# When a guard's flag is made: between the last two adds, or after them

## The chip, the cores and the metric

The kernel runs on one core of one Trainium2 chip. Its time is device microseconds of one execution, the median of several runs. Beside the times there is one profiled execution, from which every duration below is read. Engines are named TensorE (PE, its weight loads PEld), VectorE (DVE), ScalarE (ACT), GpSimd (POOL) and SyncE (SP); a "q" behind the name (SPq) marks what the engine's sequencer does: waits, branches, DMA issues and loads of a register.

## The reference

For x of 2048 tokens by 512 (bfloat16), xn = layernorm(x), and the output is the sum of three parts:

```
x
+ attention(xn)   32 heads of 16, causal, a window of 256 tokens, softmax, then wo
+ mixer(xn)       z = gelu(xn @ w_in); z1, z2 = halves of z (688 each)
                  g = w_sp @ layernorm(z2) + b_sp;   (z1 * g) @ w_out
```

## The kernel before

The tokens are tiles of 128 (`NB` = 16). A first stage normalizes x, transposes it and makes the mixer's z; a second one works through attention and the rest of the mixer, in an order written out by hand (`ORDER`): each word of it takes a few matmuls from the generators `q_work` (projections), `g_work` (w_sp times z2) and `f_work`, or one step of attention (`do_scores`, `do_mask`, `pv`, `normalize`).

`f_work(t, c0)` makes the output of token tile t: six matmuls with `w_out` (L479) and four with `wo` (L486) into one bank, then VectorE adds x to it (L491), and a store goes out (L495). The last tile, t = 15, is done in two halves of 256 columns; the second half's store is issued by ScalarE, every other by SyncE. The order ends with `f10 f10 f10`: tile 14, then the two halves of tile 15.

Attention takes the exponent without subtracting a row's maximum. Whether that was safe is checked: `check_sums` compares the reciprocals of all the sums with two bounds; for the last group it reduces to one number for each partition (`low1`, L628), and a DMA of SyncE's (L632) brings these 128 numbers into one row on one partition, kept in `rows`. After the whole order the guard follows: VectorE reduces that row (L813) and makes `flag`, 0 or 1 (L816); `nc.values_load` (L819) has each of the five engines load the flag into a register, a `TENSOR_LOAD` in its queue; and `tc.If(again > 0)` (L825) has each engine compare and branch.

Where the flag is 1, `attention_with_maximum` makes all of the output again by a second path, with a maximum subtracted, in loops. With these inputs it isn't taken: each engine jumps over it. Each semaphore that the second path would count up is counted up instead on the way around it: one `EVENT_SEMAPHORE` (L825) on TensorE, VectorE, ScalarE and GpSimd, and eight on SyncE, one for each DMA semaphore, each waiting first until all earlier DMAs on it have landed. Then the kernel ends (L850): SyncE waits for all the semaphores, and two barriers follow.

All engines run their queues in order. SyncE's last work ahead of the guard are three stores (tiles 13 and 14, first half of 15); ScalarE's is the store of the second half.

Of the kernel before, what the change touches and what calls it, by code (L numbers as in the profile page):

```python
# [8 lines left out]
P = 128  # L9
BF = mybir.dt.bfloat16  # L10
F32 = mybir.dt.float32
ACT = mybir.ActivationFunctionType
ALU = mybir.AluOpType

S_TOK = 2048
D = 512
# [9 lines left out]
NB = S_TOK // P  # L26
# [47 lines left out]
def kernel(  # L74
# [12 lines left out]
    nc = tc.nc  # L87
    x2 = A_x.flatten_outer_dims()
    out2 = out.flatten_outer_dims()
# [22 lines left out]
    flag = pers.tile([P, 1], mybir.dt.int32, name="flag")  # L112
    wspp = ctx.enter_context(tc.tile_pool(name="wspp", bufs=2))
    sm = ctx.enter_context(tc.tile_pool(name="sm", bufs=4))
# [44 lines left out]
    with ExitStack() as actx:  # L159
# [20 lines left out]
        for half in range(2):  # L180
            for k, eng in ((0, nc.sync), (1, nc.scalar)):
# [3 lines left out]
                    out=w_in_sb[:, :, f0 : f0 + HALF], in_=w_in_v[:, :, f0 : f0 + HALF]  # L185
# [5 lines left out]
        with nc.allow_non_contiguous_dma(reason="tiny bias gather"):  # L191
# [3 lines left out]
            out=w_out_sb[:, 0:5, :], in_=B_w_out[0:640, :].rearrange("(c p) n -> p c n", p=P)  # L195
# [5 lines left out]
        for _ in range(WARM):  # L201
# [7 lines left out]
            out=hmask[:],  # L209
            in_=ident[:].rearrange("p (s e d) -> p e s d", s=4, e=2),  # L210
            axis=mybir.AxisListType.XY,
# [11 lines left out]
        for h in range(2):  # L223
            part = slice(h * KB, h * KB + KB)
            nc.gpsimd.affine_select(
                out=maskFD[part, 0, :], in_=maskFD[part, 0, :], pattern=[[-1, KB]],
# [3 lines left out]
                out=maskFD[part, 1, :], in_=maskFD[part, 1, :], pattern=[[1, KB]],  # L230
# [231 lines left out]
    def load_xo(t):  # L462
        xos[t] = cp.tile([P, D], BF, name="xo", bufs=4)
        nc.sync.dma_start(out=xos[t][:], in_=x2[t * P : (t + 1) * P, :])
# [4 lines left out]
    def f_cols(t):  # L469
        return D // 2 if t == NB - 1 else D  # L470

    def f_work(t, c0):
        if c0 == 0 and t + 2 < NB:
            load_xo(t + 2)
        xo = xos[t]
        w = f_cols(t)
        fo = ps_x.tile([P, 512], F32, name="fo", tag="f")
        for ch in range(NFC):
            nc.tensor.matmul(  # L479
                fo[:, 0:w], lhsT=uTs[t][:, ch, :], rhs=w_out_sb[:, ch, c0 : c0 + w],  # L480
                start=(ch == 0), stop=False,
            )
            yield
        q0 = t % 2 * P
        for c in range(NC):
            nc.tensor.matmul(  # L486
                fo[:, 0:w], lhsT=oTs[t // 2][:, c, q0 : q0 + P], rhs=wo_sb[:, c, c0 : c0 + w],
                start=False, stop=(c == NC - 1),
            )
            yield  # L490
        nc.vector.tensor_tensor(  # L491
            out=xo[:, c0 : c0 + w], in0=fo[:, 0:w], in1=xo[:, c0 : c0 + w], op=ALU.add
        )
        eng = nc.scalar if c0 > 0 else nc.sync
        eng.dma_start(out=out2[t * P : (t + 1) * P, c0 : c0 + w], in_=xo[:, c0 : c0 + w])  # L495

# [138 lines left out]
    def attention_with_maximum(gctx):  # L635
# [5 lines left out]
        def turn(out, src, k):  # L641
            pt = ps_x.tile([P, k, P], BF, name="pt", tag="f")
            for c in range(k):
                nc.tensor.transpose(
                    out=pt[:, c, :], in_=src[:, c * P : (c + 1) * P], identity=ident[:]
                )
            nc.vector.tensor_copy(out=out[:], in_=pt[:])
# [9 lines left out]
            out=band[:], in_=band[:], pattern=[[1, NK]],  # L657
# [3 lines left out]
            out=band[:], in_=band[:], pattern=[[-1, NK]],  # L661
# [7 lines left out]
        with tc.For_i(0, NG, 1) as G:  # L669
            qx = gen.tile([P, 2, S_TOK], BF, name="qx")  # L670
            for b in range(4):
                nc.vector.tensor_copy(
                    out=qx[:, :, b * 512 : b * 512 + 512],
                    in_=qpad[b][:, bass.ds(G, 1), :, :].rearrange("p o e q -> p (o e) q"),
                )
            nc.vector.tensor_copy(
                out=kx[:, KW:], in_=kT[:, bass.ds(G, 1), :].rearrange("p o k -> p (o k)")
            )
            nc.vector.tensor_copy(
                out=vx[:, 2:, :], in_=v_y[:, :, bass.ds(G * VG, VG)]  # L680
            )
            with tc.For_i(0, NB, 1) as t:
# [3 lines left out]
                    out=keep, in0=band[:], in1=valid[:, bass.ds(t * P, NK)], op=ALU.mult  # L686
                )
                nc.vector.tensor_scalar(
                    out=minus, in0=keep, scalar1=1.0, scalar2=NEG,
                    op0=ALU.subtract, op1=ALU.mult,  # L690
                )
                nc.vector.tensor_scalar(
                    out=keep, in0=keep, scalar1=SM_SCALE, scalar2=None, op0=ALU.mult
# [6 lines left out]
                    out=qw.rearrange("p (e q) -> p e q", e=2), in_=qx[:, :, bass.ds(t * P, P)]  # L700
                )
                nc.vector.tensor_copy(out=vw, in_=vx[:, bass.ds(t, 3), :])
                op = ps_s.tile([P, 2, 512], F32, name="op", tag="S")[:, 0, 0 : 8 * VW].rearrange(
                    "p (h w) -> p h w", w=VW)
                for hh in range(8):
# [13 lines left out]
                        out=p[:], in_=sc, func=ACT.Exp, bias=top[:], scale=1.0  # L719
# [3 lines left out]
                    for k in range(3):  # L723
# [8 lines left out]
                    out=oa[:, bass.ds(t, 1), bass.ds(G * P, P)].rearrange(  # L732
                        "p o (h d) -> p (o h) d", d=DH),
                    in0=op[:, :, 0:DH], in1=rs[:].unsqueeze(2).to_broadcast([P, 8, DH]),
                    op=ALU.mult,
                )

        with tc.For_i(0, NB, 1) as t:
            row0 = t * P
            xo = cp.tile([P, D], BF, name="xo", bufs=4)  # L740
            nc.sync.dma_start(out=xo[:], in_=x2[bass.ds(row0, P), :])
            ws = wspp.tile([P, NB, P], BF, name="wspT")
            nc.sync.dma_start_transpose(out=ws[:], in_=B_w_sp[bass.ds(row0, P), :])
            u = cp.tile([P, UPAD], BF, name="u")
            nc.gpsimd.memset(u[:, FH:UPAD], 0.0)
            for j in range(2):
                gf = ps_x.tile([P, 512], F32, name="gf", tag="f")
                for c in range(NB):
                    nc.tensor.matmul(
                        gf[:, 0:HALF], lhsT=ws[:, c, :],  # L750
                        rhs=z2n[:, c, j * HALF : (j + 1) * HALF],
                        start=(c == 0), stop=(c == NB - 1),
                    )
                nc.vector.scalar_tensor_tensor(
                    out=u[:, j * HALF : (j + 1) * HALF], in0=gf[:, 0:HALF],
                    scalar=b_all[:, bass.ds(t, 1)],
                    in1=z1[:, bass.ds(t, 1), j * HALF : (j + 1) * HALF].rearrange(
                        "p o f -> p (o f)"),
                    op0=ALU.add, op1=ALU.mult,
                )  # L760
            uT = cp.tile([P, NFC, P], BF, name="uT", bufs=4)
            turn(uT, u, NFC)
            oT = cp.tile([P, NC, P], BF, name="oT1", tag="u")
            ot = cp.tile([P, D], BF, name="ot1", tag="uT", bufs=4)
            nc.vector.tensor_copy(
                out=ot[:], in_=oa[:, bass.ds(t, 1), :].rearrange("p o d -> p (o d)")
            )
            turn(oT, ot, NC)
            fo = ps_x.tile([P, 512], F32, name="fo", tag="f")
            for c in range(NFC):  # L770
                nc.tensor.matmul(
                    fo[:], lhsT=uT[:, c, :], rhs=w_out_sb[:, c, :], start=(c == 0), stop=False
                )
            for c in range(NC):
                nc.tensor.matmul(
                    fo[:], lhsT=oT[:, c, :], rhs=wo_sb[:, c, :],
                    start=False, stop=(c == NC - 1),
                )
            nc.vector.tensor_tensor(out=xo[:], in0=fo[:], in1=xo[:], op=ALU.add)
            nc.sync.dma_start(out=out2[bass.ds(row0, P), :], in_=xo[:])  # L780

    rows = []
    masks = [(J, g, i) for J, g in pairs for i in range(3)]
    units = list(pairs)
    load_cross(0)
    work = {
        "q": [(4, q_work(b, i)) for b, i in qkv_list],
        "g": [(NB, g_work(t, j)) for t in range(NB) for j in range(2)],
        "f": [(NFC + NC, f_work(t, c0)) for t in range(NB) for c0 in range(0, D, f_cols(t))],
    }  # L790
    left = 0
    for step in ORDER.split():
# [16 lines left out]
            if left == 0:  # L809
                assert next(unit, None) is None  # L810
    assert not (left or groups or masks or units or later or any(work.values()))
    low = sm.tile([P, 1], F32, name="low")
    nc.vector.tensor_reduce(  # L813
        out=low[0:1, :], in_=rows[0][0:1, :], axis=mybir.AxisListType.X, op=ALU.min
    )
    nc.vector.tensor_scalar(  # L816
        out=flag[0:1, :], in0=low[0:1, :], scalar1=0.5, scalar2=None, op0=ALU.is_lt
    )
    again = nc.values_load(  # L819
        flag[0:1, 0:1], min_val=0, max_val=1,  # L820
        skip_runtime_bounds_check_because="a comparison gives 0 or 1",
    )
    late_ctx.close()
    ep_ctx.close()
    with tc.If(again > 0):  # L825
        with ExitStack() as gctx:
            attention_with_maximum(gctx)

# [26 lines left out]
```

## Time and profile before

| | |
|---|---|
| median of three runs | 258.57 us (258.11 to 258.86) |
| profiled execution | 258.24 us, its span 256.4 us |
| granted TensorE clock | 1.000 |
| busy share of the span | TensorE 97%, ScalarE 74%, VectorE 70%, GpSimd 6% |
| instructions | 9109 |
| DMA | 25.38 MB, of it 0.60 MB of instructions |

The span runs from the first to the last instruction of the program; the time of an execution has some 1.8 us around it. Starts are counted from the span's start. A group of instructions is shown with its line, engine, operation and count, then the shortest, middle and longest duration in ns and when the first and last of them started. The chain of waits goes back from the last piece of work to what released it, and is shown in order of time: start, duration, what. The view of the DMA queues gives packets, MB and the time that the packets took as a share of 16 DMA engines over the stretch asked for; its line "DMA" cuts that stretch into 40 slices and shows the busy share in tenths.

### The profile page before, as it was taken

To read this page: it belongs to the slowest core of one execution; us is meant where nothing else is said; L and a number is where in the kernel's file an instruction comes from. 1 tells how busy PE (TensorE), PEld (TensorE's weight loads), DVE (VectorE), ACT (ScalarE), POOL (GpSimd) and SP (SyncE) were. 2 spreads that over 40 slices of the span, in tenths; PEclk is the share of its full clock that TensorE was granted. 3 is DMA by queue.
4 is the path that set the end of the run, shared out by engine and by line. 5 is a ranking of instruction groups with operands and counts; after the bars stand their busy time and mean duration, and the time that the engine had idled before them with its cause. 6 is when DMAs were issued, how large, how long until landed. Compare 5 with 4: busy or idle time off the path is not lost.

```text
span 256.4 us, 9109 instructions
## 1 busy us (share of the span) xinstructions
PE 249.9 (97%) x4053; PEld 137.4 (54%) x4053; DVE 178.8 (70%) x370; ACT 190.7 (74%) x228; POOL 16.6 (6%) x52
## 2 busy tenths in 40 slices
PE   6999999999999999999999999999999999999993
PEld 2665555555555455464555564556465546465552
DVE  4796997885566758844679857385577877488983
ACT  2777536546546998989898889898988888986800
POOL 4120311211010100000000000000000000000000
PEclk9999999999999999999999999999999999999999
DMA  6994020026201206396843936465469193563032
GB/s 206 393 243 146 0 64 20 0 51 140 58 0 42 66 4 115 72 140 112 153 72 71 187 70 111 93 117 115 41 151 155 48 150 80 117 108 64 20 95 68
DMA packets 65786, 25.38 MB, mean 99 GB/s; under 512 B 53664, under 2 KB 65232, under 8 KB 65744
## 3 DMA queue, kind: packets, MB, share of 16 engines
q1 hardware_dynamic: 64256, 23.74, 44.4%
q10 hardware_dynamic: 1488, 1.03, 1.4%
q8 instruction: 32, 0.52, 0.9%
q14 instruction: 10, 0.08, 0.1%
HBM read 8.41 MB, written 2.10 MB: 41 GB/s over the span
## 4 chain that ended last, share of the span: by engine, by line
PE 96%; DVE 1%; DMA 1%; POOL 0%; issue 0%
PE gf L443 32%; PE zp L292 15%; PE S L580 10%; PE fo L479 9%; PE S L523 8%; PE pj_o L129 6%; PE fo L486 6%; PE pj_f L129 5%; PE pj_f L147 3%; PE pj_o L147 3%; DMA xt<-in_A_x_dram 1%; PE tp L282 1%; DVE stats L240 1%; POOL rs L250 0%; DVE xo L491 0%; DVE xn L268 0%
## 5 line engine op out<-in xcount | busy, mean ns | idle before, releaser
L589 ACT ACTIVATE E<-S 128x1024 bf16<-128x1024 f32 x152 | 141.2, 1025 | 16.1 <-PE S L580 15.8
L443 PE MATMUL gf<-z2n,wspT 128*128 128x344 bf16 x512 | 86.5, 310 | 0.0
L443 PEld LDWEIGHTS <-wspT 128*128 128x128 bf16 x512 | 45.5, 98 | 32.3 <-issue 11.6
L608 DVE TENSOR_TENSOR E<-E,maskFD 128x1024 bf16<-128x1024 bf16 (+2 forms) x48 | 38.4, 808 | 5.9 <-ACT E L589 5.4
L292 PE MATMUL zp<-w_in_sb,xnT 128*128 128x344 bf16 x256 | 41.7, 309 | 0.0
L292 PEld LDWEIGHTS <-xnT 128*128 128x128 bf16 x256 | 24.9, 98 | 15.1
L580 PE MATMUL S<-qpad,kT 32*64 32x512 bf16 (+3 forms) x960 | 31.9, 309 | 0.0
L530 DVE STREAM_TRANSPOSE ot<-S 128x1024 f32<-128x1024 f32 x16 | 19.9, 1244 | 16.7 <-PE S L523 16.5
L449 DVE SCALAR_TENSOR_TENSOR u<-gf,b_all,z 128x344 bf16<-128x344 f32 x32 | 18.3, 571 | 17.9 <-PE gf L443 15.6
L479 PE MATMUL fo<-w_out_sb,uT 128*128 128x512 bf16 (+1 forms) x102 | 24.4, 367 | 0.0
L299 ACT ACTIVATE z<-zp 128x688 bf16<-128x688 f32 x16 | 11.9, 745 | 15.1 <-PE zp L292 15.0
L580 PEld LDWEIGHTS <-kT 32*64 32x64 bf16 x960 | 10.8, 102 | 21.2 <-issue 20.2
L523 PE MATMUL S<-E,v_y 64*32 64x256 bf16 (+2 forms) x960 | 21.8, 231 | 0.0
L523 PE MATMUL S<-E,vx 64*32 64x256 bf16 (+3 forms) x960 | 21.8, 232 | 0.0
L523 PEld LDWEIGHTS <-vx 64*32 64x32 bf16 x960 | 18.4, 90 | 4.1 <-issue 3.7
L523 PEld LDWEIGHTS <-v_y 64*32 64x32 bf16 x960 | 19.2, 90 | 0.6 <-issue 0.6
L299 ACT ACTIVATE z2n<-zp 128x688 bf16<-128x688 f32 x16 | 11.9, 745 | 10.1 <-PE zp L292 10.1
L129 PEld LDWEIGHTS <-wqkv 128*128 128x128 bf16 x128 | 12.5, 98 | 12.4
L129 PE MATMUL pj_o<-xnT,wqkv 128*128 128x512 bf16 x72 | 18.5, 379 | 0.0
L140 DVE TENSOR_SCALAR qpad<-qt,hmask 128x512 bf16<-128x512 bf16 x32 | 9.7, 345 | 11.4 <-ACT qt L138 11.4
L486 PE MATMUL fo<-wo_sb,oT 128*128 128x512 bf16 (+1 forms) x68 | 17.3, 368 | 0.0
L491 DVE TENSOR_TENSOR xo<-fo,xo 128x512 bf16<-128x512 f32 (+1 forms) x17 | 11.1, 654 | 8.4 <-PE fo L486 8.1
(60 smaller groups left out, 197.2 us busy)
## 6 DMA issues: line engine op xcount, KB each, us to landing
xo<-in_A_x_dram SPq DMA_DIRECT2D x16, 128.0 KB, 3.5
out_dram<-xo SPq DMA_DIRECT2D x15, 128.0 KB, 2.2
vx<-v_y SPq DMA_DIRECT2D x16, 102.0 KB, 3.2
xt<-in_A_x_dram SPq DMA_DIRECT2D x3, 512.0 KB, 9.7
wqkv<-in_A_wqkv_dram SPq DMA_DIRECT2D x1, 1536.0 KB, 10.5
w_in_sb<-in_B_w_in_dram ACTq DMA_DIRECT2D x2, 344.0 KB, 5.8
w_in_sb<-in_B_w_in_dram SPq DMA_DIRECT2D x2, 344.0 KB, 6.0
w_out_sb<-in_B_w_out_dram SPq DMA_DIRECT2D x1, 640.0 KB, 5.6
```

Source lines behind the costliest of these rows:

```text
L129: nc.tensor.matmul(pt[:], lhsT=wqkv[:, c, w0 : w0 + P], rhs=xnT[:, c, t0 : t0 + 512], start=(c == 0), stop=(c == NC - 1),)
L292: nc.tensor.matmul(zp[:, j, 0:HALF], lhsT=xnT[:, c, n * P : (n + 1) * P], rhs=w_in_sb[:, c, f0 : f0 + HALF], start=(c == 0), stop=(c == NC ...
L299: nc.scalar.activation(out=dst.rearrange("p (j f) -> p j f", j=2), in_=zp[:, :, 0:HALF], func=ACT.Gelu_apprx_tanh,)
L443: nc.tensor.matmul(gf[:, 0:HALF], lhsT=wspT[t][:, c, :], rhs=z2n[:, c, j * HALF : (j + 1) * HALF], start=(c == 0), stop=(c == NB - 1),)
L449: nc.vector.scalar_tensor_tensor(out=u[:, j * HALF : (j + 1) * HALF], in0=gf[:, 0:HALF], scalar=b_all[:, t : t + 1], in1=z1[:, t, j * HALF ...
L479: nc.tensor.matmul(fo[:, 0:w], lhsT=uTs[t][:, ch, :], rhs=w_out_sb[:, ch, c0 : c0 + w], start=(ch == 0), stop=False,)
L486: nc.tensor.matmul(fo[:, 0:w], lhsT=oTs[t // 2][:, c, q0 : q0 + P], rhs=wo_sb[:, c, c0 : c0 + w], start=False, stop=(c == NC - 1),)
L523: nc.tensor.matmul(o[32 * s : 32 * s + 32, h, q0 : q0 + ni * KB], lhsT=v, rhs=Et[part, s, e, c0 : c0 + ni * KB], start=(i == 0), stop=(i = ...
L530: nc.vector.transpose(out=ot[:].rearrange("p h b j -> p (h b j)"), in_=o[:].rearrange("p h c -> p (h c)"))
L580: nc.tensor.matmul(o.rearrange("p (e q) -> p e q", e=2)[:, :, c0 - b0 : c0 - b0 + ni * KB], lhsT=kT[32 * s : 32 * s + 32, 2 * g + h, k0 : ...
L589: nc.scalar.activation(out=Et[:, 2 * i : 2 * i + 2, :, b0 : b0 + w].rearrange("p s e q -> p (s e) q"), in_=S[i][:].rearrange("p s (e q) -> ...
L608: nc.vector.tensor_tensor(out=v, in0=v, in1=mask, op=ALU.mult)
```

## The change

The reduce and the compare that make the flag move from behind the whole order into `f_work`: for the last half tile they are issued after its matmuls and ahead of its add. The load of the flag by the five engines moves there too, behind that add and ahead of that store's issue. So in each queue: VectorE has reduce, compare, add, load; ScalarE the load, then the store; TensorE the load behind its last matmul; SyncE behind its last store. In the second path two lines change: the load of x and the store of the output in its last loop go from SyncE's queue to ScalarE's, which then holds three DMAs of that path, with the transposes it had.

```diff
@@ f_work
             yield
+        last = t == NB - 1 and c0 + w == D
+        if last:
+            low = sm.tile([P, 1], F32, name="low")
+            nc.vector.tensor_reduce(
+                out=low[0:1, :], in_=rows[0][0:1, :], axis=mybir.AxisListType.X, op=ALU.min
+            )
+            nc.vector.tensor_scalar(
+                out=flag[0:1, :], in0=low[0:1, :], scalar1=0.5, scalar2=None, op0=ALU.is_lt
+            )
         nc.vector.tensor_tensor(
             out=xo[:, c0 : c0 + w], in0=fo[:, 0:w], in1=xo[:, c0 : c0 + w], op=ALU.add
         )
+        if last:
+            again.append(nc.values_load(
+                flag[0:1, 0:1], min_val=0, max_val=1,
+                skip_runtime_bounds_check_because="a comparison gives 0 or 1",
+            ))
         eng = nc.scalar if c0 > 0 else nc.sync
         eng.dma_start(out=out2[t * P : (t + 1) * P, c0 : c0 + w], in_=xo[:, c0 : c0 + w])
@@ attention_with_maximum, its last loop
-            nc.sync.dma_start(out=xo[:], in_=x2[bass.ds(row0, P), :])
+            nc.scalar.dma_start(out=xo[:], in_=x2[bass.ds(row0, P), :])
...
-            nc.sync.dma_start(out=out2[bass.ds(row0, P), :], in_=xo[:])
+            nc.scalar.dma_start(out=out2[bass.ds(row0, P), :], in_=xo[:])
@@ at the end
+    again = []
...
-    low = sm.tile([P, 1], F32, name="low")
-    nc.vector.tensor_reduce(
-        out=low[0:1, :], in_=rows[0][0:1, :], axis=mybir.AxisListType.X, op=ALU.min
-    )
-    nc.vector.tensor_scalar(
-        out=flag[0:1, :], in0=low[0:1, :], scalar1=0.5, scalar2=None, op0=ALU.is_lt
-    )
-    again = nc.values_load(
-        flag[0:1, 0:1], min_val=0, max_val=1,
-        skip_runtime_bounds_check_because="a comparison gives 0 or 1",
-    )
     late_ctx.close()
     ep_ctx.close()
-    with tc.If(again > 0):
+    with tc.If(again[0] > 0):
```

## The prediction

> **What bounds the kernel now.** The page first: its chain is TensorE (96%) from the start to the last matmul, and no edit touches a matmul. So I read the end only, first with the chain of waits of the last microseconds, then with the groups of the flag's load (L819) and of the branch (L825).
>
> ```profile
> 252.12 0.45 PE fo L486 x4
> 252.57 0.02 issue
> 252.60 0.42 DVE xo L491
> 253.02 0.19 DVE low L813
> 253.21 0.02 issue
> 253.23 0.14 DVE flag L816
> ```
> ```profile
> L819 SPq TENSOR_LOAD <-flag x1: 488/488/488, 253.4 to 253.4; - x1
> L819 DVEq TENSOR_LOAD <-flag x1: 542/542/542, 253.4 to 253.4; - x1
> L819 PEldq TENSOR_LOAD <-flag x1: 497/497/497, 253.4 to 253.4; - x1
> ```
> ```profile
> L825 SPq EVENT_SEMAPHORE  x8: 17/17/17, 254.5 to 255.1; - x8
> L825 SPq COMPARE_BRANCH  x1: 57/57/57, 254.0 to 254.0; - x1
> ...
> L825 PEldq COMPARE_BRANCH  x1: 368/368/368, 254.0 to 254.0; - x1
> ```
>
> Read as a chain: last add to 253.02, reduce, flag to 253.37, five loads of some 0.5 us to 253.9, branches at 254.0. SyncE then jumps (254.02 to 254.50) and, where the second path is left out, counts up eight DMA semaphores in turn (L825), one about every 0.07 us; eight waits (L850, 255.13 to 255.59), a drain and two barriers follow, to the end at 256.43. After the last add this looks like a pure chain of the guard, 1.0 us from 253.02 to the branch. It is not the only one.
>
> The last store is ScalarE's (L495): issued at 253.05, when the add is done, and landed 1.56 us later, at 254.62 (the group of L495 in that stretch; the page's row says 1.6). By the program, SyncE's second count-up waits on just that store's semaphore. In the trace the eight start at 254.50, 254.63, 254.72, 254.80, 254.86 ...: the second comes 0.13 us after the first, where the others are 0.07 to 0.09 apart, and 0.02 after the landing. So at the end two chains arrive within 0.06 us: the guard's, and the store's landing.
>
> The third view is of the DMA queues, in the store's stretch (253.2 to 254.9, first line) and in the last 1.5 us (254.9 to 256.4, the other two).
>
> ```profile
> q10 hardware_dynamic: 144, 0.07, 13.1%
> ```
> ```profile
> q14 instruction: 3, 0.02, 5.6%
> q8 instruction: 1, 0.02, 5.3%
> ```
>
> The store's 128 packets of 512 bytes and 16 of 4 bytes run from 253.93 to 254.26 (packet records), on all 16 DMA engines. The four instruction fetches start at 255.05, 255.07, 255.11 and 255.20: 1.0 to 1.2 us after the branches, no other instruction packet being near. The one on q8 is TensorE's (32 such packets of 16 KB for its 8,100 instructions) and occupies one DMA engine for 1.28 us; those on q14 have 8 KB and take 0.3 to 0.55 us. Now they start 0.4 us after the store has landed, and harm nobody.
>
> **The change, step by step.** Times are those of the profiled execution: 258.24 us, 256.43 of it span, so 1.8 us lie around the span; the median of the runs is 258.57, 0.33 more. I add the change to each.
>
> *Reduce and flag ahead of the last add.* VectorE waits for TensorE from 251.93 to 252.60 (the last add's 0.7 us of idle). The row of minima lands at 249.63 + 1.98 = 251.61. In the trace the reduce starts 0.085 before the recorded end of the add ahead of it (252.94 against 253.02); after the first half's add (251.50 to 251.93) it would start at 251.84: + 0.26 + 0.035 + 0.14, flag at 252.28. The last add is ready at 252.60, so 0.31 us of cover is left and the edit costs nothing. Were the row late, the add would be queued behind it: free up to a landing at about 252.15.
>
> *The loads.* TensorE, GpSimd and SyncE start theirs at 252.32 (0.03 to 0.04 after the flag, as now; SyncE's own store is issued until 252.29), are done at 252.81, and branch at 252.9: 1.1 us earlier. TensorE's load stands behind its last matmul in the queue (dispatched by 252.29). ScalarE's stands ahead of its store, and the store is who waits behind it: done at 252.80, the add at 253.02, so 0.2 us of cover; the store still goes at 253.05 and ScalarE's branch at 253.48 (0.5 earlier). VectorE's load stands behind the last add: 253.06 to 253.60, branch at 253.68 (0.35 earlier); if the load does not wait for the add's end, 0.4 earlier still, and nobody waits for VectorE until 255.44.
>
> *What that brings on the path.* SyncE reaches its first count-up at 253.43 instead of 254.50, waits there for its own store (landing 253.48), and at the second for ScalarE's at 254.62. The start of that count-up moves from 254.63 to 254.63. Without the landing it would have come at 254.57: the gain is bounded between 0 and 0.06 us. Of 1.1 us removed from the guard's chain, the store's landing keeps all but that; what is late next is the landing.
>
> *The two DMAs of the second path.* The path isn't taken. Between branch and target SyncE has some instructions less and ScalarE some more; the eight count-ups are all SyncE's though ScalarE's own transposes of that path are among what they make up for, so I leave them there: 0. Bounds: three count-ups moved would save 3 x 0.07 = 0.2 us, three more cost 0.2.
>
> *What the earlier branches trigger.* The fetches move with the branches: SyncE's 8 KB (branch 252.89 + 1.09) to 253.98, TensorE's 16 KB (252.93 + 1.09) to 254.02, both among the store's packets (253.93 to 254.26); ScalarE's and VectorE's come at 254.5 and later. The trace shows once what such a fetch does to a transfer on its DMA engine: at 245.85 TensorE fetches for 1.56 us while a load of x (L464) and a store are under way. The other engines are through with the load by 247.1; then, in the stretch 247.15 to 248.35,
>
> ```profile
> DMA  0000000020020002000200200020020000010000
> ...
> q1 hardware_dynamic: 14, 0.01, 5.7%
> ```
>
> one engine alone works off packets, one per 0.11 us, from 247.40, right at the fetch's end. That load lands after 3.83 us, another in a quiet stretch (234.82) after 2.14; the store after 3.63 against 1.5 to 1.9 for those at the end. So I read: a fetch holds its engine's packets until it is over.
>
> [...] By the other reading, that transfers simply interleave at small grain, the sum would be 0.
>
> Price for the store: when the fetch starts at 254.02, 3 of the 8 packets on that engine are gone. The fetch takes 0.89 us (shortest row, at 236.89, nothing beside it) to 1.56; it ends at 254.91 to 255.58. Five packets at 0.03 (their pitch now) to 0.11 us: 255.05 to 256.1. From the store's last packet to its landing 0.38 us: 255.4 to 256.5 instead of 254.62, so +0.8 to +1.9 us. With SyncE's 8 KB alone (0.31 to 0.64 us): +0.2 to +1.0. With no overlap: 0. I take +1.0, near the low end of the first, since little else moves at that time, as in the shortest row. All that follows the second count-up moves along: sum 0 (matmuls, adds) - 0 (guard) + 1.0 (landing) = 259.2 for the profiled execution, 259.5 against the median.
>
> **The rivals.** Less than 0.3%, 0.78 us here, a measurement of this kernel can hardly tell from no change (its three runs lie 0.75 apart).
>
> *The fetch misses the store.* The store is the bound, but TensorE's load starts only when its matmuls are through (252.56 instead of 252.32), or the fetch follows later than 1.09 us: from 0.24 us later on it finds the store's packets gone. Then 258.5 (-0.06 to 0), or up to 259.1 if only the 8 KB fetch meets it. For it: the margin is just 0.24 us. Against: loads on other engines start 0.04 after the flag, and sequencer instructions run ahead of their engine (VectorE's waits at L491 do).
>
> *The landing stops being the bound: faster.* If the moved DMAs change who makes the count-ups, or their order, so that the wait for the last store comes last instead of second, seven count-ups and most of the eight waits run before the landing: 14 x 0.065 = 0.9 us, giving 257.6. Each place saves 0.065 us, so it tells from twelve places later on (0.78 us). Against: all eight are SyncE's now, although both engines issue DMAs there.
>
> *The row is late.* From a landing at 252.15 the last add waits; each microsecond more is one on the end. At the 3.6 us that a disturbed store took, it lands at 253.25, the flag comes at 253.7 and the add 1.1 us late: 259.7. Against: only stores of 1.5 to 1.9 us are near it.
>
> [...]
>
> **How the numbers follow.** Fetch holds the store: 0.47 (nearly all of it over 0.78 us; own range 259.3 to 260.5). Fetch misses it, or an 8 KB one alone meets it: 0.33, within 0.3% almost always. Landing wait moved back: 0.13, nearly all counted as faster, the rest of its places and of the runs' scatter going to the same. Row late: 0.07, half of it over 0.3%. Sums: slower 0.51, same 0.37, faster 0.12. The range for 8 in 10 runs from 258.1 (fetch misses, and runs scatter by 0.3) to 260.5 (the dear end of the fetch); left out is most of the faster case and the tail of a late row.
>
> **What would show it.** In the changed profile: L819 loads at 252.3 on four engines and about 253.06 on VectorE; the last add still right behind the last matmul; the store of L495 issued 0.45 us after the add's start as now, but landing after 2.3 us or more instead of 1.6; instruction packets at 254.0 among the store's; SyncE's second count-up right behind the landing, and 1.8 us from there to the end. Wrong it is if the store lands after 1.6 us again (then no change), if the last add or its store starts later (then row or ScalarE's load), or if the count-ups are fewer or in another order.

## The result, and the profile after

| | before | after |
|---|---|---|
| median of 6 runs | 258.31 us | 259.86 us |
| ratio, 95% interval | | 1.0055 (1.0041 to 1.0068) |
| profiled execution | 258.24 us | 259.98 us |
| its span | 256.4 us | 258.3 us |

The change makes the kernel 1.4 us slower (0.0055 x 258.3; the interval is 1.1 to 1.8; the two medians alone would give 1.55), in spite of a guard that is through 1.0 to 1.1 us earlier. The timeline shows that the whole front part went as planned (start, duration, engine, line, operation):

```profile
252.15 0.14 DVE L497 TENSOR_SCALAR flag<-low 1x1 int32<-1x1 f32 x1
252.61 0.42 DVE L500 TENSOR_TENSOR xo<-fo,xo 128x256 bf16<-128x256 f32 x1 [0.31 <-PE fo L486]
253.06 0.36 ACTq L509 DMA_DIRECT2D out_dram<-xo  x1
```

The flag is there at 252.29 instead of 253.37; the last add stands at 252.61 and the last store at 253.06, both 0.01 later than before. The groups of the loads (L504, formerly L819) and of the branch (L829, formerly L825):

```profile
L504 PEldq TENSOR_LOAD <-flag x1: 492/492/492, 252.3 to 252.3; - x1
L504 SPq TENSOR_LOAD <-flag x1: 537/537/537, 252.3 to 252.3; - x1
L504 DVEq TENSOR_LOAD <-flag x1: 541/541/541, 252.6 to 252.6; - x1
```
```profile
L829 SPq EVENT_SEMAPHORE  x8: 17/17/17, 253.5 to 256.9; - x8
...
L829 PEldq COMPARE_BRANCH  x1: 373/373/373, 252.9 to 252.9; - x1
L829 SPq COMPARE_BRANCH  x1: 58/58/58, 253.0 to 253.0; - x1
```

Branches at 252.9 and 253.0 instead of 254.0. But SyncE's eight count-ups, which took 0.6 us before (254.5 to 255.1), now stretch from 253.5 to 256.9: the first is at 253.50, the second only at 256.46. It waits for the last store, which landed at 256.44, and that store's own group says why:

```profile
L509 ACTq DMA_DIRECT2D out_dram<-xo x1: 358/358/358, 253.1 to 253.1; - x1
...
DMA to landing us min/median/max: 3.4/3.4/3.4
```

It took 3.38 us from issue to landing, where it was 1.56: 1.82 us more, and the span grew by 1.83. The DMA queues in the same stretch as in the prediction (253.2 to 254.9):

```profile
q10 hardware_dynamic: 135, 0.06, 12.3%
q14 instruction: 3, 0.02, 5.1%
q8 instruction: 1, 0.02, 5.0%
```

All four instruction fetches now start in it, where there was none; and of the store's 144 packets nine are missing. The nine are in the stretch 255.2 to 256.0, which is cut here into slices of 0.02 us:

```profile
DMA  0000000020020020200020010102000000000000
...
q10 hardware_dynamic: 9, 0.00, 4.5%
```

One packet at a time is worked off, from 255.37 on, as by one DMA engine alone (the records do not name the engine; eight packets of 512 bytes and one of 4 are its share of the store, 144 / 16, and the store counts its semaphore up 16 times: 14 times by 254.71, then at 255.57 and at 256.44). TensorE's fetch of 16 KB began at 254.03 and took 1.35 us: to 255.38. The chain of waits does not show any of this: it still ends with the last add, 5.2 us ahead of the end, since it follows engines, and what came last is a transfer.

### The profile page after: what moved, and what is told of

Read it like the earlier page. It is cut to its first block, busy times and chain, and to the rows that moved or that the text cites. A ratio compares the mean times of both kernels' runs of the same rounds, so it can differ in the third digit from the quotient of the medians.

```text
span 258.3 us, 9085 instructions
## 1 busy us (share of the span) xinstructions
PE 248.0 (96%) x4029; PEld 137.3 (53%) x4053; DVE 178.8 (69%) x370; ACT 190.5 (74%) x228; POOL 16.6 (6%) x52
## 4 chain that ended last, share of the span: by engine, by line
PE 94%; DVE 1%; DMA 1%; issue 1%; POOL 0%
PE gf L443 31%; PE zp L292 15%; PE S L594 10%; PE S L537 8%; PE fo L479 8%; PE pj_o L129 6%; PE fo L486 6%; PE pj_f L129 5%; PE pj_o L147 3%; PE pj_f L147 3%; DMA xt<-in_A_x_dram 1%; PE tp L282 1%; DVE stats L240 1%; POOL rs L250 0%; DVE xo L500 0%
## 5 line engine op out<-in xcount | busy, mean ns | idle before, releaser
L479 PE MATMUL fo<-w_out_sb,uT 128*128 128x512 bf16 (+1 forms) x88 | 22.2, 365 | 1.1 <-issue 0.6
```

What stands on the lines that cost most here:

```text
L479: nc.tensor.matmul(fo[:, 0:w], lhsT=uTs[t][:, ch, :], rhs=w_out_sb[:, ch, c0 : c0 + w], start=(ch == 0), stop=False,)
```

## The experiments

The theory: a branch of TensorE or SyncE is followed, about 1.1 us later (1.08 to 1.17 in the eleven profiles that have fetches), by a fetch of instructions; a fetch that meets the last store's packets holds its DMA engine's share of them until it is over; SyncE's second count-up waits for that landing, and with it the end. The rivals: the two DMAs moved in the second path; ScalarE's load ahead of its store; the early guard as such. Ratios are to the kernel before, over 4 to 12 executions; fetches and landings are of the one profiled execution of each kernel.

**The flag without the moved DMAs, and the moved DMAs without the flag.** In the first, both lines of the second path stay with SyncE; in the second, only they change.

```diff
-            nc.scalar.dma_start(out=xo[:], in_=x2[bass.ds(row0, P), :])
+            nc.sync.dma_start(out=xo[:], in_=x2[bass.ds(row0, P), :])
...
-            nc.scalar.dma_start(out=out2[bass.ds(row0, P), :], in_=xo[:])
+            nc.sync.dma_start(out=out2[bass.ds(row0, P), :], in_=xo[:])
```

> The flag early and loaded early, the second path's two DMAs left in SyncE's queue. Theory (an instruction fetch that follows the early branches holds the last store's packets on its DMA engine): as slow as the whole change, 1.4 to 1.8 us over the kernel before, the store landing 3.0 to 3.6 us after its issue. Rival (the two DMAs moved in the second path make the difference): no change, the store landing after 1.6 us.

> The kernel before with only the second path's two DMAs moved to ScalarE's queue. All theories: no change (within 0.1 us), SyncE's eight count-ups as before; a difference would be one of code placement.

The flag alone: 1.0073 (1.0047 to 1.0098), the store landing after 3.00 us. The DMAs alone: 0.9997 (0.9985 to 1.0009), with SyncE's eight count-ups as before and the landing after 1.56 us. The first rival has fallen.

**ScalarE's order.** The load is issued behind the store.

```diff
-        if last:
-            again.append(nc.values_load(...))
         eng = nc.scalar if c0 > 0 else nc.sync
         eng.dma_start(out=out2[t * P : (t + 1) * P, c0 : c0 + w], in_=xo[:, c0 : c0 + w])
+        if last:
+            again.append(nc.values_load(...))
```

> The whole change, but the load of the flag is issued behind the last store, so that only ScalarE's order changes: store, then load. Theory: TensorE and SyncE still branch at 252.9 to 253.0, their fetches start at 254.0, and it is as slow as the change, +1.4 to +1.8 us. Rival (ScalarE's load ahead of its store slows the store): no change.

The ratio is 1.0066 (1.0047 to 1.0085); the store lands after 2.99 us, and TensorE's fetch begins 0.97 us after the store's issue, as in the change. ScalarE's load has no part in it that shows.

**The same, and the flag 0.3 us later.** To the kernel just shown one line is added: the reduce of the row is made twice.

```diff
             nc.vector.tensor_reduce(
                 out=low[0:1, :], in_=rows[0][0:1, :], axis=mybir.AxisListType.X, op=ALU.min
             )
+            nc.vector.tensor_reduce(
+                out=low[0:1, :], in_=rows[0][0:1, :], axis=mybir.AxisListType.X, op=ALU.min
+            )
```

> As the kernel with the load behind the last store, but VectorE reduces the row twice, which makes the flag 0.30 us later (252.59 instead of 252.29); nothing else differs. Theory: the fetches start at 254.33 instead of 254.03, 0.1 us after the store's last packet, the store lands after 1.6 us, and 0.3 us of extra work take 1.4 to 1.8 us off: within 0.1 us of the kernel before. Rival (the early guard itself, or its order in the queues, costs the time): still +1.4 to +1.8 us.

The ratio is 0.9988 (0.9977 to 0.9999): one instruction more takes the whole loss away. The DMA view from 253.6 to 254.4, in slices of 0.02 us, shows the store's packets as one block, and the fetches as single 9s behind it:

```profile
DMA  0000255699999987531109000900009000000000
```

The fetches of SyncE and TensorE begin 1.22 and 1.29 us after the store's issue; the store's last packet of data begins 1.18 after, and its very last, of 4 bytes, ends at 1.215. So the first fetch clears it by 0.01 us, where I had expected 0.1. The store lands after 1.57 us. So neither the early guard nor its place costs anything, only the moment of the fetch. That this kernel comes out 0.3 us below the one before is not explained: from the store's issue to the end it has 3.39 us, the kernel before 3.38, and the interval all but touches 1.

**Which fetch.** To the change a second flag is added, made behind the last add, and some engines load that one; the others load the early one, and each branches on what it loaded. The cut is shown for TensorE and SyncE late; the other two kernels have TensorE alone, or SyncE alone, in the second list. `mybir.EngineType.` is left out of the names here.

```diff
+                flag[0:1, 0:1], engines=[Pool, Activation, DVE], ...
...
+            nc.vector.tensor_scalar(
+                out=flag2[0:1, :], in0=low[0:1, :], scalar1=0.5, scalar2=None, op0=ALU.is_lt
+            )
...
+    again.append(nc.values_load(
+        flag2[0:1, 0:1], engines=[PE, SP], ...
```

> The whole change, but TensorE and SyncE load a second flag, made behind the last add as before; ScalarE, VectorE and GpSimd load the early one, ScalarE still ahead of its store. Theory: the two fetches that met the store start about 255.0 again, the store lands 1.5 to 1.7 us after its issue, and the time is within 0.1 us of the kernel before. Rival (ScalarE's load ahead of its store slows the store): as slow as the change, +1.4 to +1.8 us.

> The whole change, but TensorE alone loads a second flag made behind the last add; SyncE's 8 KB fetch is left among the store's packets, TensorE's 16 KB one is not. Theory with a size for each fetch (a fetch holds its engine until it is over): the held packets go 0.6 us after the fetch's start, the store lands 2.0 to 2.4 us after its issue instead of 1.6, the time is 0.4 to 0.8 us over the kernel before. Rival (any fetch met costs the same, or only both together): +1.5 us, or 0.

> The whole change, but SyncE alone loads a second flag made behind the last add; TensorE's 16 KB fetch is left among the store's packets. Theory: the landing is held as long as in the change (2.9 to 3.4 us after issue), since the longer fetch ends last; SyncE comes 1.1 us later than in the change, still ahead of the landing: +1.4 to +1.8 us. Rival (SyncE's early waiting or its fetch makes the loss): no change, or half of it.

| kernel | ratio (95%) | TensorE's fetch | SyncE's fetch | held packets go | landing |
|---|---|---|---|---|---|
| before | 1 | +2.06 | +2.0 | none held | 1.56 |
| the change | 1.0055 (1.0041 to 1.0068) | +0.97, 1.35 | +0.99, 0.59 | +1.57 and +2.31 | 3.38 |
| TensorE and SyncE late | 0.9989 (0.9977 to 1.0001) | +2.06 | +2.0 | none held | 1.57 |
| TensorE late | 1.0032 (1.0019 to 1.0045) | +2.07 | +0.99, 0.59 | +1.57 | 2.27 |
| SyncE late | 1.0071 (1.0055 to 1.0086) | +0.99, 1.37 | +2.0 | +2.35 | 3.43 |

All times are in us from the store's issue, a fetch with its duration behind the comma (packet records; SyncE's fetch is told by its branch, 1.1 us before it). In each row the held packets start again within 0.02 us of the fetch's end (0.99 + 0.59 = 1.58; 0.97 + 1.35 = 2.32; 0.99 + 1.37 = 2.36), and they are eight of 512 bytes for each fetch, the whole share of one engine of sixteen (128 / 16), never a part of it. The kernel with SyncE late, in the stretch 255.0 to 256.6:

```profile
DMA  0008000000500000005000000001011101000100
...
q14 instruction: 3, 0.02, 4.8%
q10 hardware_dynamic: 9, 0.00, 2.2%
```

The 8 and the two 5s are 8 KB fetches, which met nothing; the ones at the right are the nine packets that were behind TensorE's 16 KB. TensorE's fetch alone makes the whole loss, and SyncE's 8 KB alone makes 0.8 us (0.5 to 1.2). The rival "any fetch costs the same" has fallen: the longer fetch costs more, and the landing comes 0.98 to 1.08 us after the end of TensorE's in the four kernels where it met the store, 0.69 after SyncE's where that one met it alone.

**No jump, no fetch.** The second path's code is left out of this kernel: where the flag is 1, VectorE only writes a small tile.

```diff
     with tc.If(again[0] > 0):
-        with ExitStack() as gctx:
-            attention_with_maximum(gctx)
+        nc.vector.memset(warm[:], 0.0)
```

> The whole change with the early guard, but the second path's code is left out: where the flag is 1, VectorE only writes a small tile. The jump is then a few instructions long and SyncE has no count-ups. Theory (the fetch comes from a jump into another block of code): no instruction packets near the last store although the branches come at 252.9, the store lands after 1.6 us, and the end comes 1.24 us after the landing instead of 1.8: 0.5 to 0.6 us below the kernel before. Rival (the early guard costs 1.5 us with or without a fetch): about 1 us over it.

All DMA queues from 250 on:

```profile
q1 hardware_dynamic: 576, 0.33, 17.3%
q10 hardware_dynamic: 144, 0.07, 3.7%
```

There is no instruction packet, though TensorE and SyncE branch at 253.2, 0.1 us ahead of the store's issue, as in the change; and the store lands after 1.57 us, with the end 1.26 after it. So the fetch belongs to the jump over the second path's code: the same early branches without it bring none. The time falls by less than I expected: 0.9990 (0.9981 to 0.9999), 0.26 us instead of 0.5 to 0.6. In its profile the store goes 0.26 us later than in the kernel before and the rest is 0.55 shorter; whether the part ahead of it is later as a rule here stays open. Over all the profiled executions whose kernels have the same stores, that issue lies anywhere from 252.82 to 253.75, so 0.26 us in a single one says little.

**A version that beats both.** With the fetch out of the way, what the guard saves ahead is lost again at SyncE's second count-up. Two kernels put the last store's semaphore in the eighth place: in the trace of the kernel before, its 106 DMAs count up the eight semaphores in turn, the last one the second of them, and with six stores more it is the eighth. One has the early flag with the reduce made twice, the other is the kernel before.

```diff
         eng = nc.scalar if c0 > 0 else nc.sync
-        eng.dma_start(out=out2[t * P : (t + 1) * P, c0 : c0 + w], in_=xo[:, c0 : c0 + w])
+        n = 2 if t < 6 else 1
+        for i in range(n):
+            a, b = c0 + i * w // n, c0 + (i + 1) * w // n
+            eng.dma_start(out=out2[t * P : (t + 1) * P, a:b], in_=xo[:, a:b])
```

> As the kernel that reduces the row twice, and the stores of the first six token tiles go in two DMAs each, which moves the last store's semaphore from the second to the last place among SyncE's eight count-ups. Theory: SyncE makes seven count-ups while the store is under way and only the eighth waits for the landing; 6 x 0.067 = 0.4 us less between landing and end (1.4 instead of 1.8), 0.4 to 0.5 us below the kernel before. Rival (the twelve half stores cost more on the way than is saved, or the place makes no difference): 0, or slower.

> The kernel before, with the stores of the first six token tiles in two DMAs each, so that the last store's semaphore stands last among SyncE's eight count-ups; the guard stays late. Theory (two chains end together, the guard's and the landing's): SyncE now arrives at its first count-up at 254.50 and, unhindered, at the eighth at 255.02, 0.04 us earlier than before: no change (0 to -0.1 us); the gain of the kernel with the early guard needs both. Rival (the place alone makes the gain): -0.4 us.

With the early flag the ratio is 0.9983 (0.9974 to 0.9993), 0.4 us below the kernel before, and the median 257.92 (258.35 for the kernel before in the same series); with the late one it is 1.0001 (0.9991 to 1.0010), though the two intervals just meet. In the profile of the late one the store lands 1.55 us after its issue and the eighth count-up stands at 1.97: there the guard's chain holds the end, and the place gives 0.04 us from issue to end, as expected. The group of count-ups with the early flag:

```profile
L835 SPq EVENT_SEMAPHORE  x8: 17/17/17, 254.5 to 255.5; - x8
```

Seven are made by 254.97, with the store still under way (it lands at 255.49), and the eighth at 255.50; from the store's issue to the end it is 3.03 us, in the kernel before 3.38 and in the change 5.20. Against the kernel that only makes the reduce twice, the two intervals overlap, so the place itself is shown by the profiles (3.03 us from issue to end against 3.39) rather than by the times.

## Why the prediction was right, and where its size was off

*Reduce and flag.* Flag forecast at 252.28, found at 252.29; the last add right behind its matmul. The 0.31 us of cover was there: VectorE's idle time ahead of the last add fell from 0.7 to 0.31.

*Loads and branches.* TensorE's load forecast at 252.32, found at 252.33; SyncE's branch at 252.89, found at 252.96 (its load took 0.54 instead of 0.49). ScalarE's load ended at 252.80 with its store at 253.06, as forecast. VectorE's load did not wait for the end of the add that runs ahead of it (252.62, not 253.06): the second of the two values given; nobody waited for it. On every queue the starts at the end keep the program's order: on VectorE reduce 251.85, flag 252.15, add 252.61, load 252.62, branch 253.24; on ScalarE load 252.32, store 253.06, branch 253.45; on TensorE last matmul 252.30, load 252.33, branch 252.93.

*The landing is next.* SyncE stood at its first count-up at 253.50 (forecast 253.43) and then waited 2.9 us for the store. The two DMAs of the second path: 0, shown by the run that moves them alone.

*The fetch.* Its start was forecast at 254.02 (TensorE) and 253.98 (SyncE), and found at 254.03 and 254.05. It met the store, which the prediction gave a chance of 0.47. That was close: TensorE's fetch began 0.1 us after the store's first packet, and SyncE's, 0.24 us later in the kernel with two reduces, met nothing. The reading that the prediction took from the row at 245.85 held: the held packets started within 0.02 us of the fetch's end in every run in which a fetch met the store. The other one, interleaving at a small grain, would have let some of the eight go in the 0.59 to 1.37 us that the fetches took; none went. Why they wait no run shows.

*The size.* The sum had +1.0 (bounds 0.8 to 1.9); the change measured +1.4 (1.1 to 1.8) and +1.83 in the profiled execution. Three terms were small. The cheap end of the sum took the shortest fetch, 0.89 us, because little else moves at the end; it took 1.35 here and 0.93 to 1.37 in the four runs in which TensorE's met the store, so "quiet" did not make it short. The nearer row was at hand: the same fetch, of the same engine after the same branch, took 1.28 us in the kernel before, and there it met nothing. What sets its length stays open. I had 3 of the 8 packets gone when it starts; none was, though the store had been running 0.1 us on other engines: 8 packets took 0.38 us, where 5 were to take 0.15 at the cheap end. And from the start of the last data packet to the landing it was 0.69 us behind TensorE's fetch, in all four runs, against the 0.38 that I carried over from the kernel before. So 0.46 us more of fetch, 0.23 of packets and 0.31 of landing come on top of that end's 0.82: 1.82, the measured delay of the landing. Only the last term lay outside what the sum allowed for; that the sum stayed under 1.9 it owes to the other two, which were below their dear ends.

*The rivals.* The fetch did not miss the store: the load was not held until the matmuls were through. The 0.24 us of margin named there was real: 0.3 us of delay is all that the kernel with two reduces adds. The wait for the landing did not move among the count-ups; where I moved it, the forecast mechanism held, with 0.35 us in the profile for six places (0.39 by the forecast's 0.065 for each). The row landed at 251.62, on time. After the jump every engine ran on 0.1 to 0.5 us after the end of its branch, as before, and ahead of any fetch of its own.

## What to carry to other kernels

In this kernel a fetch of instructions began 1.08 to 1.17 us after TensorE's and SyncE's branch over the second path's code, and each fetch that met the last store held eight of its packets of 512 bytes until within 0.02 us of the fetch's end, the fetch taking 0.59 to 1.37 us: look for packets of the instruction queues next to the transfer that the end waits for, and keep the two apart, by delaying the branch if need be. Where two chains end together, ask of a gain on one what the other still holds, and look for a landing as the last link, which a chain of waits through engines does not show (here it ended 5.2 us ahead of the end). Where one wait in a row of small ones comes last, try it in the last place: here, from the second place to the eighth, it took 0.35 us off in the profile (3.03 us from the store's issue to the end against 3.38).

## What the runs showed of the hardware that I had not expected

Behind a fetch of 16 KB, the store's held packets of 512 bytes came 0.04 to 0.07 us apart in the change (0.02 behind SyncE's 8 KB), and the landing 0.69 us after the start of the last (in the change from 2.69 to 3.38 us after issue). Behind SyncE's 8 KB alone it came 0.53 us after, undisturbed 0.37 to 0.39; in the kernel with the store's semaphore in the last place, where a fetch begins 0.003 us after the store's last packet ends, it was 0.45. Why the landing is later behind a fetch stays open.

A fetch that starts 0.1 us after a store's first packet on other engines still came ahead of all eight packets of one engine, in all five runs in which a fetch met the store.
